# A cosine block loaded as 128 rows, half of each row product evicted by ScalarE and added on GpSimd, and the first transposes and one routing moved

## The chip, the cores and the metric

The kernel runs on one NeuronCore of one Trainium2 chip. Its engines are TensorE (PE; PEld is its weight load), VectorE (DVE), ScalarE (ACT), GpSimd (POOL) and SyncE (SP, which here only issues DMAs). Each takes its own instructions in the order in which they were written for it and waits on semaphores for the others. The metric is the device time of one execution in microseconds.

## The reference

For x of 2048 tokens and 512 features the output is a sum of three parts:

```
xn  = layernorm(x)
A   = C @ (xn @ Wre.T) - S @ (xn @ Wim.T)        # real part of a 2-D Fourier transform; C, S: 2048 x 2048 cosines, sines
q   = xn @ w_q                                   # 32 heads, two halves of 128 each
s1, s2 = q[:, :, :128] @ k1.T, q[:, :, 128:] @ k2.T        # 64 scores a half
top 2 of s1 + top 2 of s2 -> 4 candidates, best 2 -> gates g (softmax), expert indices e
B   = sum over heads and both experts of g * gelu(xn . u[e]) * v[e]   # 4096 experts
out = x + A + B
```

## The kernel before

**Layout.** Tokens are ordered so that four quarters of the sequence fold onto each other; a group g is 128 rows of each quarter, and groups are taken in the order G = (1, 0, 2, 3). Matrices named c (A in the code) are blocks of the cosine (k = 0) and sine (k = 1) matrices for one group, 128 rows of 1024 numbers, loaded by load().

**Start (to about 63 us).** For each group the layernorm is done (ln_a: statistics; ln_b: scale on ACT at L376), the quarters are folded on DVE (fold_t L412, fold_d L395 to L406, the results zq at L430 and L431), and main(k, g) multiplies the fold with the block c: eight fp32 matmuls of PE at L451 (four pairs p_00, p_10, p_01, p_11). k = 0 runs over all groups, then k = 1. Between them PE transposes the normalised rows of a group (xpose_a, L514, into banks xp; ACT copies them out at L517; xpose_b adds the low part, L525 and L527). The product of the first weights with the keys (tiles m, L145) lies in the same four PSUM banks as the first transposes until m_keep copies it out on ACT (L590). For k = 1 the block of group 0 was loaded in three pieces: 127 rows (L305), half of row 0 (L306), and the other half of row 0 from another array (row512, L296).

**Scores (63 to about 440 us).** Eight chunks j of four heads; in each, PE makes the scores of 16 token tiles i (L962, twelve matmuls into one of four banks pa), ACT copies them out (L967), DVE takes the top values (L970, L974). In between PE makes the next chunk's weights (m_mul, L141, banks of pools pc and pb, two each), from halves that ACT (L155, L160) and POOL (L163) split. The routing of a chunk (candidates, gates, indices) is done in the next chunk in three parts: part 0 (POOL L807 to L812, DVE L810, L811), part 2 (indices, POOL L829 on, DVE L826 on) and part 1, which begins with an exponential on ACT (L815). In chunk 1 the parts follow scores 9, 11 and 13 (LAG) and are held behind that score's matmuls; in the later chunks they follow scores 1, 2 and 4 and are not held.

**Row products (103 to 182 us).** Nine calls of hid put one 128-row piece each of the Fourier result in a bank (hy, pools pc and pb). Columns 0 to 256 are real parts; ACT evicts them in five pieces (L557 to L561). Columns 257 to 511 are the imaginary parts, which DVE reads from PSUM and adds to and subtracts from the real ones (L564, L565). The table HID names the score behind which each call comes: one at score 13 of chunk 0, the last at score 0 of chunk 2. y_store writes the results to DRAM ten scores later; for two of the tiles one half has rows 1 to 127 alone.

**What sets the order.** The code writes each engine's stream through a scheduler that orders instructions by its own estimate; pace, behind, hold and follow add orderings without waits between engines. The order of the queues is therefore read from the built program.

Of the kernel before, what the change touches and what calls it, by code (L numbers as in the profile page):

```python
# [16 lines left out]
ALU = mybir.AluOpType  # L17
AX = mybir.AxisListType

P = 128  # L20
# [16 lines left out]
def tile_fnet_peer(ctx, tc, x, ca, cb, c5, wt, wf, wr, wq, kt, ut, vn, uv, out):  # L37
# [257 lines left out]
    def row512(k, dst, eng=nc.sync):  # L295
        eng.dma_start(dst.rearrange("p (k c) -> p k c", k=4),  # L296
                      cb[k, 0, 4 * k:4 * k + 4, 0:1, 6:8].rearrange("k p b c -> p k (b c)"))

    def load(k, g):

        t = A[k, g] = raw_tile(f"c{k}_{g}").rearrange("p a t -> p (a t)") if k else vf[g]
        if k == 0 or g:
            nc.sync.dma_start(t, ca[k, g])
            return
        nc.sync.dma_start(t[1:P], ca[k, g, 1:P])  # L305
        nc.sync.dma_start(t[0:1, 0:512], ca[k, g, 0:1, 0:512])  # L306
        row512(k, t[0:1, 512:1024])

# [132 lines left out]

    def main(k, g, after=None):

        first, last = g == G[0], g == G[-1]
        if first:
            PP[k] = [[pa(f"p{k}_{dt}{h}") for h in range(2)] for dt in range(2)]
        for h in range(2):
            r = A[k, g][:, h * 512:(h + 1) * 512]
            l = Q[k][g][:, h ^ k]
            for dt in range(2):  # L450
                i = nc.tensor.matmul(PP[k][dt][h], l[:, dt * P:(dt + 1) * P], r, start=first, stop=last)  # L451
                if after is not None:
                    pace(i, after)

# [46 lines left out]
    XP = {}  # L501
    XL = {}

# [4 lines left out]
    def xpose_a(i, sub, after=None):  # L508

        p = XP[i] = (pb if sub and i // 4 % 2 else pc)(f"xp{i}")  # L510
        src = xn[i % 4][:, i // 4]
        for kd in range(KD):
            c = slice(kd * P, (kd + 1) * P)
            XL[0] = nc.tensor.matmul(p[:, c], src[:, c], ident, start=kd == 0, stop=kd == KD - 1 and not sub,  # L514
                                     is_transpose=True, skip_group_check=True)
        pv = p.rearrange("p (k n) -> p k n", k=KD)
        hi = nc.scalar.activation(xt[i][:, 0], pv, AF.Copy, scale=XS)  # L517
        if after is not None:
            pace(hi, after)
# [29 lines left out]

    def hid(t, n, pre, pn, pim, bank):  # L550

        nc.tensor.matmul(bank[:n, 0:129], pre[0], wfs[:, 0:129], start=True, stop=False)
        nc.tensor.matmul(bank[:n, 0:129], pn, wrs, start=False, stop=True)
        nc.tensor.matmul(bank[:n, 129:257], pre[1], wfs[:, 129:257], start=True, stop=True)
        nc.tensor.matmul(bank[:n, 257:384], pim[0], wfs[:, 257:384], start=True, stop=True)
        nc.tensor.matmul(bank[:n, 384:512], pim[1], wfs[:, 384:512], start=True, stop=True)
        nc.scalar.activation(t[:, 2:256:2], bank[:n, 0:127], AF.Copy)  # L557
        nc.scalar.activation(t[:, 1:256:2], bank[:n, 129:257], AF.Copy)
        nc.scalar.activation(t[:, 256:258], bank[:n, 127:129], AF.Copy)
        nc.scalar.activation(t[:, 513:514], bank[:n, 127:128], AF.Copy)  # L560
        nc.scalar.activation(t[:, 0:1], bank[:n, 128:129], AF.Copy)  # L561
        for a, b, im in ((2, 259, bank[:n, 257:384]), (1, 258, bank[:n, 384:512])):
            e = slice(a, 256, 2)
            nc.vector.tensor_tensor(t[:, b:513:2], t[:, e], im, op=ALU.add)  # L564
            nc.vector.tensor_tensor(t[:, e], t[:, e], im, op=ALU.subtract)  # L565

# [14 lines left out]
    for g in G:  # L581
        load(1, g)
    wfs = uf[14][:, 0:512]
# [13 lines left out]
    for n, g in enumerate(G):  # L597
# [9 lines left out]
        if n in (1, 2):  # L607
            fold_t(0, g)
            ln_a(G[n + 1], n + 1)
            if n == 1:  # L610
                OWN.append(m_keep((0, 2), ln_x(G[3], 3, SQ[2])))
            fold(0, g, AG[n + 1], lambda i: ln_b(G[n + 1], n + 1, i))
        else:
            fold(0, g)
        if n in (1, 2):
            for q in (0, 1) if n == 1 else (2, 3):
                xpose_a(4 * q + G[0], True, LN[n + 1])
        if n == 1:
            m_keep((1, 3), LN[2])
        main(0, g, XL[0] if n == 1 else None)  # L620
        if n == 0:
# [62 lines left out]
    def y_rows(n):  # L684

        if n == 8:
# [5 lines left out]
        hid(uf[n][:, 0:514], P, [PT[0][dt][h][:, c] for dt in range(2)], p256[:, h, c],  # L692
            [PT[1][dt][h][:, c] for dt in range(2)], (pb if q else pc)(f"hy{q}_{g}"))

    def y_store(n):
        if n == 8:
            t, a, b, r = uf[13][0:1, 264:778], y_d[8][0:1], y_d[12][0:1], slice(0, 1)
# [5 lines left out]
        nc.sync.dma_start(b[:, 0:256], t[r, 258:514])  # L703
        nc.sync.dma_start(b[:, 256:512], t[r, 0:256])

# [6 lines left out]
    def part_b(safe, stS, stP, stE, xt, u_sb, cmp_p):  # L712
# [316 lines left out]
        for j in range(NCH):  # L1029
# [8 lines left out]
            for i in range(NT):  # L1038
# [643 lines left out]
```

## Time and profile before

| what | us |
|---|---|
| runs of the kernel | 1081.33, 1085.77, 1083.87 (median 1083.87) |
| the profiled execution | 1083.84 |
| its span, first to last instruction | 1081.9 |
| TensorE clock granted, mean | 0.996 |
| PE busy / DVE / ACT / POOL | 1054.7 / 958.0 / 729.2 / 625.3 |

Times inside the span are counted from its start. A row of the timeline gives start, length, engine, line, operation, output and inputs, and in brackets how long the engine stood idle ahead of it and what ended that. A row of the windows gives a stretch, its length, busy time (and instructions) of PE, PEld, DVE, ACT and POOL, the granted clock of TensorE (1.00 is full), the share of the 16 DMA engines and GB/s. A row of the groups gives the count, busy time and mean length in ns, or least, median and greatest.

### The profile page before, as it was taken

The numbers are of one execution on the slowest core, as the hardware profiler recorded it, in microseconds if no ns is written. First come the engines' busy times: TensorE is split into PE (matmuls) and PEld (weight loads), VectorE is DVE, ScalarE is ACT, GpSimd is POOL, SyncE is SP. The second block draws the span as 40 slices with busy tenths as digits, with TensorE's granted clock in tenths as the row PEclk, the third lists the DMA queues.
The fourth block names the chain that finished last, engine by engine and source line by source line (L and its number), as shares of the span: only waits on it lengthen the run. The fifth ranks groups of instructions, "written<-read, shape, count | busy, mean of one in ns | idle before, by whom it ended". The sixth has DMA issues, their size and how long they took to land.

```text
span 1081.9 us, 28392 instructions
## 1 busy us (share of the span) xinstructions
PE 1054.7 (97%) x11005; PEld 688.2 (64%) x11005; DVE 958.0 (89%) x2720; ACT 729.2 (67%) x1359; POOL 625.3 (58%) x574
## 2 busy tenths in 40 slices
PE   6899998999999999999999999999999999999997
PEld 5344554454544544996785968769587685867853
DVE  7969779879999999988999998999899997999871
ACT  5787656778788757445776667666657775777641
POOL 1145646688797946225756576556566665666622
PEclk9999999999999999999999999999999999999999
DMA  8268185435445341277866767675687767666611
GB/s 334 87 152 238 64 316 174 151 136 194 156 157 184 119 137 67 86 247 223 253 192 193 214 201 231 211 233 182 189 245 210 224 209 234 213 211 212 190 31 53
DMA packets 96376, 198.87 MB, mean 184 GB/s; under 512 B 23618, under 2 KB 38999, under 8 KB 96232
## 3 DMA queue, kind: packets, MB, share of 16 engines
q1 hardware_dynamic: 75338, 125.65, 35.4%
q0 software_dynamic: 20736, 71.31, 22.5%
q8 instruction: 88, 1.44, 0.5%
q14 instruction: 56, 0.46, 0.1%
q10 hardware_dynamic: 158, 0.01, 0.0%
HBM read 176.65 MB, written 17.10 MB: 179 GB/s over the span
## 4 chain that ended last, share of the span: by engine, by line
PE 80%; DVE 8%; DMA 5%; POOL 3%; issue 2%; ACT 1%; SPq 0%; ACTq 0%; DVEq 0%; POOLq 0%
PE s L962 25%; PE z L1131 24%; PE v L1196 23%; PE g L1168 4%; DMA c<-in_ca_dram 3%; PE m L141 2%; DVE vals L970 2%; DVE idx L974 1%; PE p L451 1%; POOL ov L1256 1%; DMA wq<-in_wq_dram 1%; DVE L L1155 1%; DMA cx<-in_ca_dram 1%; DMA u<-in_c_dram 0%; POOL ga L1222 0%
## 5 line engine op out<-in xcount | busy, mean ns | idle before, releaser
L962 PE MATMUL s<-m,xq 128*128 128x512 f16 x1536 | 339.3, 380 | 0.0
L1131 PE MATMUL z<-xb,u 128*128 128x128 f16 x5376 | 306.8, 219 | 1.6 <-DVE y L1211 1.6
L1131 PEld LDWEIGHTS <-u 128*128 128x128 f16 x5376 | 301.5, 98 | 4.5 <-issue 1.6
L1196 PE MATMUL v<-v,act 128*128 128x512 f16 x1344 | 296.5, 379 | 0.0
L1256 POOL TENSOR_TENSOR ov<-ov,ga 128x512 f32<-128x512 f32 x128 | 182.5, 1426 | 184.3 <-ACT ga L1251 113.4
L962 PEld LDWEIGHTS <-xq 128*128 128x128 f16 x1536 | 148.7, 98 | 173.9 <-issue 2.6
L1196 PEld LDWEIGHTS <-act 128*128 128x128 f16 x1344 | 128.9, 98 | 149.2
L1222 POOL DMA_INDIRECT ga<-in_uv_dram,eix x128 | 160.5, 1254 | 46.2 <-POOL ov L1256 35.7
L970 DVE MAX8 vals<-ss 128x8 f32<-128x64 f32 x1024 | 152.7, 216 | 17.3 <-ACT ss L967 17.3
L1155 DVE TENSOR_TENSOR L<-io_lam,cmp 128x2048 f16<-128x2048 f16 x112 | 155.0, 1399 | 11.5 <-PE g L1168 11.4
L1134 ACT ACTIVATE act<-z,scl 128x512 f32<-128x512 f32 x112 | 75.4, 679 | 61.8 <-PE z L1131 61.3
L974 DVE FIND_INDEX8 idx<-vals,ss 128x8 uint16<-128x256 f32 x256 | 107.2, 419 | 0.0
L967 ACT ACTIVATE ss<-s,wsc 128x512 f32<-128x512 f32 x112 | 75.4, 679 | 43.4 <-PE s L962 33.9
L1251 ACT ACTIVATE ga<-ga,za 128x512 f32<-128x512 f32 x128 | 92.3, 721 | 10.1 <-ACT za L1249 0.7
L944 ACT ACTIVATE cx<-cx 128x896 f32<-128x896 f32 x64 | 60.6, 946 | 48.1 <-DVE cx L924 29.6
L1184 ACT ACTIVATE act<-g 128x1024 f16<-128x1024 f32 x56 | 73.1, 1308 | 23.5 <-DVE g L1179 23.1
L1238 DVE SCALAR_TENSOR_TENSOR ga<-ga,px 128x512 f32<-128x512 f32 x128 | 85.7, 677 | 0.1
L1187 DVE TENSOR_TENSOR act<-g,act 128x1024 f16<-128x1024 f32 x56 | 72.9, 1303 | 11.6 <-ACT act L1184 10.6
L1179 DVE SCALAR_TENSOR_TENSOR g<-act,scl,g 128x1024 f32<-128x1024 f32 x56 | 71.4, 1278 | 3.2 <-ACT act L1134 1.8
L918 POOL TENSOR_TENSOR cx<-cx 128x512 f32<-128x512 f32 (+2 forms) x48 | 53.8, 1140 | 14.0 <-DMA cx<-in_cb_dram 14.0
L918 DVE TENSOR_TENSOR cx<-cx 128x512 f32<-128x512 f32 (+2 forms) x61 | 48.5, 828 | 14.1 <-DMA cx<-in_cb_dram 14.0
L1168 PEld LDWEIGHTS <-L 128*128 128x128 f16 x1792 | 51.8, 96 | 8.5 <-DVE L L1155 1.7
(300 smaller groups left out, 1309.6 us busy)
## 6 DMA issues: line engine op xcount, KB each, us to landing
cx<-in_cb_dram SPq DMA_DIRECT2D x50, 448.0 KB
wq<-in_wq_dram SPq DMA_DIRECT2D x32, 512.0 KB
fit<-in_wq_dram SPq DMA_DIRECT2D x28, 512.0 KB
uv<-in_ut_dram SPq DMA_DIRECT2D x16, 512.0 KB
uv<-in_vn_dram SPq DMA_DIRECT2D x16, 512.0 KB
cx<-in_cb_dram SPq DMA_DIRECT2D x28, 224.0 KB
xt_d<-xq SPq DMA_DIRECT2D x16, 256.0 KB
xb<-xt_d SPq DMA_DIRECT2D x14, 256.0 KB
```

The costliest lines, as they stand in the source:

```text
L918: v_eng.tensor_tensor(v, v, tv[:, 0:1].to_broadcast([P, len(ix), 256]), op=o)
L962: mm = nc.tensor.matmul(ps, xt[i][:, l, kd, :], m[:, r, kd, :], start=(n == 0), stop=(n == 3 * KD - 1))
L970: nc.vector.max(vals[:, i, w, :, h], s[:, g, :])
L974: nc.vector.max_index(idx[:, i, w].rearrange("p k h -> p (k h)"), vals[:, i, w, 0:2].rearrange("p k h -> p (k h)"), s[:, w * HC:g + 1, :]. ...
L1131: mm = nc.tensor.matmul(p[:, cc * P:(cc + 1) * P], ug[:, l, c % 2, kd, :], xb[:, r, kd, :], start=(n == 0), stop=(n == 3 * KD - 1))
L1155: nc.vector.tensor_tensor(L.rearrange("p t (l two) -> p t l two", two=2), io_lam.rearrange("p (l two) -> p l two", two=2).unsqueeze(1).to_ ...
L1168: i = nc.tensor.matmul(p[:, hf, t * NC:(t + 1) * NC], L[:, t, :], R[:, hf * 16 + t, :], start=True, stop=True)
L1196: mm = nc.tensor.matmul(pv, w16[:, c, :, l], vg[:, r, c % 2, :], start=(c == 0 and k == 0), stop=(c == NC - 1 and k == 2))
L1222: nc.gpsimd.indirect_dma_start(out=t, out_offset=None, in_=uv, in_offset=bass.IndirectOffsetOnAxis(ap=eix[:, n].rearrange("p k h -> p (k h ...
L1238: nc.vector.scalar_tensor_tensor(t, t, 1.0, T["x"], op0=ALU.mult, op1=ALU.mult, accum_out=T["z", n][:, s:s + 1])
L1251: nc.scalar.activation(t, t, AF.Copy, scale=z)
L1256: T["a"] = nc.gpsimd.tensor_tensor(o, o, t, op=ALU.add)
```

## The change

Four things. The 127-row load becomes one of 128 rows, like the other blocks; row512 then overwrites half of row 0, placed behind the load of the last group. In hid, for the eight full tiles, ACT copies columns 257 to 511 of the bank into the free part of the same tile (s), and the four additions run on POOL from there. The transposes of the first group come after the third group's statistics instead of beside the second's, and all four copies of m_keep go with them. The routing that runs in chunk 2 follows scores 9, 11 and 13 and is held, as in chunk 1. Stores of rows 1 to 127 are split at row 64.

```diff
     def load(k, g):
         t = A[k, g] = raw_tile(f"c{k}_{g}").rearrange("p a t -> p (a t)") if k else vf[g]
-        if k == 0 or g:
-            nc.sync.dma_start(t, ca[k, g])
-            return
-        nc.sync.dma_start(t[1:P], ca[k, g, 1:P])
-        nc.sync.dma_start(t[0:1, 0:512], ca[k, g, 0:1, 0:512])
-        row512(k, t[0:1, 512:1024])
+        return nc.sync.dma_start(t, ca[k, g])
...
     for g in G:
-        load(1, g)
+        last = load(1, g)
+    pace(row512(1, A[1, 0][0:1, 512:1024]), last)
...
-    def hid(t, n, pre, pn, pim, bank):
+    def hid(t, n, pre, pn, pim, bank, s=None):
...
-        for a, b, im in ((2, 259, bank[:n, 257:384]), (1, 258, bank[:n, 384:512])):
+        im, eng = bank[:n, 257:512], nc.vector
+        if s is not None:
+            nc.scalar.activation(s, im, AF.Copy)
+            im, eng = s, nc.gpsimd
+        for a, b, v in ((2, 259, im[:, 0:127]), (1, 258, im[:, 127:255])):
             e = slice(a, 256, 2)
-            nc.vector.tensor_tensor(t[:, b:513:2], t[:, e], im, op=ALU.add)
-            nc.vector.tensor_tensor(t[:, e], t[:, e], im, op=ALU.subtract)
+            eng.tensor_tensor(t[:, b:513:2], t[:, e], v, op=ALU.add)
+            eng.tensor_tensor(t[:, e], t[:, e], v, op=ALU.subtract)
...
             if n == 1:
-                OWN.append(m_keep((0, 2), ln_x(G[3], 3, SQ[2])))
+                OWN.append(ln_x(G[3], 3, SQ[2]))
+            else:
+                m_keep(range(KD), SQ[3])
+                for q in (0, 1):
+                    xpose_a(4 * q + G[0], True, LN[2])
             fold(0, g, AG[n + 1], lambda i: ln_b(G[n + 1], n + 1, i))
...
-        if n in (1, 2):
-            for q in (0, 1) if n == 1 else (2, 3):
-                xpose_a(4 * q + G[0], True, LN[n + 1])
-        if n == 1:
-            m_keep((1, 3), LN[2])
-        main(0, g, XL[0] if n == 1 else None)
+        if n == 2:
+            for q in (2, 3):
+                xpose_a(4 * q + G[0], True, LN[3])
+        main(0, g)
...
-            r = slice(0 if g else 1, P)
-            t, a, b = uf[n][:, 0:514], y_d[4 * q + g], y_d[4 * q + 8 + g][r]
+            rows = [slice(0, P)] if g else [slice(1, 64), slice(64, P)]
+            t, a, b = uf[n][:, 0:514], y_d[4 * q + g], y_d[4 * q + 8 + g]
...
-                if j == 1 and not safe:
+                if j in (1, 2) and not safe:
                     if i in LAG:
```

What this makes of the queues, at three places. SP's loads of the sine blocks (c_1, c_0, c_2, c_3 are those of groups 1, 0, 2, 3), before:

```order
L303 DMA c_1_184<-in_ca_dram 128x1024
L305 DMA c_0_186<-in_ca_dram 127x1024
L306 DMA c_0_186<-in_ca_dram 1x512
L296 DMA c_0_186<-in_cb_dram 1x4x128
L303 DMA c_2_190<-in_ca_dram 128x1024
L303 DMA c_3_192<-in_ca_dram 128x1024
L584 DMA u_127<-in_wf_dram 128x512
```

and now:

```order
L302 DMA c_1_184<-in_ca_dram 128x1024
L302 DMA c_0_186<-in_ca_dram 128x1024
L302 DMA c_2_188<-in_ca_dram 128x1024
L302 DMA c_3_190<-in_ca_dram 128x1024
L296 DMA c_0_186<-in_cb_dram 1x4x128
L581 DMA u_127<-in_wf_dram 128x512
```

One load of 128 rows takes the place of two, and the half row from the other array (L296) goes behind the load of group 3.

ACT in the start, from the last step of the statistics of group 3 (mvs) on; m are the products that m_keep copies, xq_102 and xq_103 the rows of groups 2 and 3 that are normalised, xp the transposes of the first group. Before:

```order
L339 ACTIVATE mvs<-sx_317 128x1
L590 ACTIVATE u_115<-m_0_196 128x512
L338 ACTIVATE mvs<-sx_317 128x1
L590 ACTIVATE u_116<-m_2_252 128x512
L376 ACTIVATE xq_102<-xq_102,negm,rstd 128x512 x4
L517 ACTIVATE xq_101<-xp_343 128x512
L517 ACTIVATE xq_101<-xp_349 128x512
L590 ACTIVATE u_115<-m_1_199 128x512
L590 ACTIVATE u_116<-m_3_255 128x512
L353 ACTIVATE sm_369<-mvs,eps 128x4
L376 ACTIVATE xq_103<-xq_103,negm,rstd 128x512 x4
```

and now:

```order
L371 ACTIVATE xq_102<-xq_102,negm,rstd 128x512
L333 ACTIVATE mvs<-sx_316 128x1
L371 ACTIVATE xq_102<-xq_102,negm,rstd 128x512 x3
L348 ACTIVATE sm_352<-mvs,eps 128x4
L587 ACTIVATE u_115<-m_0_195 128x512
L587 ACTIVATE u_115<-m_1_198 128x512
L587 ACTIVATE u_116<-m_2_251 128x512
L587 ACTIVATE u_116<-m_3_254 128x512
L509 ACTIVATE xq_101<-xp_358 128x512
L509 ACTIVATE xq_101<-xp_364 128x512
L371 ACTIVATE xq_103<-xq_103,negm,rstd 128x512 x4
```

The normalisation of group 2 and the square root of group 3 (sm) move ahead of all four copies of m. On PE, nine transposes of group 0 (before, six) now stand between the two halves of main(1, 0).

ACT at the start of chunk 2, from the eviction of score 0 (ss_0) and the last row product (hy_3) on. Before:

```order
L967 ACTIVATE ss_0_2013<-s_0_2000,wsc 128x512
L557 ACTIVATE u_120<-hy_3_2025 128x127
L558 ACTIVATE u_120<-hy_3_2025 128x128
L559 ACTIVATE u_120<-hy_3_2025 128x2
L560 ACTIVATE u_120<-hy_3_2025 128x1
L561 ACTIVATE u_120<-hy_3_2025 128x1
L815 ACTIVATE c_0_2070<-c_0_2068 128x64
L182 ACTIVATE m_2419,sums<-m_1665 128x2048
L967 ACTIVATE ss_1_2053<-s_1_2040,wsc 128x512
```

and now:

```order
L967 ACTIVATE ss_0_2023<-s_0_2010,wsc 128x512
L549 ACTIVATE u_120<-hy_3_2035 128x127
L550 ACTIVATE u_120<-hy_3_2035 128x128
L551 ACTIVATE u_120<-hy_3_2035 128x2
L552 ACTIVATE u_120<-hy_3_2035 128x1
L553 ACTIVATE u_120<-hy_3_2035 128x1
L556 ACTIVATE u_120<-hy_3_2035 128x255
L182 ACTIVATE m_2390,sums<-m_1669 128x2048
L967 ACTIVATE ss_1_2064<-s_1_2051,wsc 128x512
```

The exponential of the routing (L815) is gone from here; it now stands ahead of the eviction of score 13. The copy of the bank's second half (L556) is new, and the four DVE additions for this tile are gone from DVE's queue and stand on POOL's.

More of the change, by code (lines that the diff above doesn't have):

```diff
@@ L440, in tile_fnet_peer, with main @@
     PP = {}
-    def main(k, g, after=None):
+    def main(k, g):
         first, last = g == G[0], g == G[-1]
@@ L450, in main @@
             for dt in range(2):
-                i = nc.tensor.matmul(PP[k][dt][h], l[:, dt * P:(dt + 1) * P], r, start=first, stop=last)
-                if after is not None:
-                    pace(i, after)
+                nc.tensor.matmul(PP[k][dt][h], l[:, dt * P:(dt + 1) * P], r, start=first, stop=last)
     def main_row():
@@ L513, in xpose_a @@
             c = slice(kd * P, (kd + 1) * P)
-            XL[0] = nc.tensor.matmul(p[:, c], src[:, c], ident, start=kd == 0, stop=kd == KD - 1 and not sub,
-                                     is_transpose=True, skip_group_check=True)
+            nc.tensor.matmul(p[:, c], src[:, c], ident, start=kd == 0, stop=kd == KD - 1 and not sub,
+                             is_transpose=True, skip_group_check=True)
         pv = p.rearrange("p (k n) -> p k n", k=KD)
```

12 lines of the change are left out of this document (6 added, 6 removed).

## The prediction

> **What bounds the kernel now.** I read the page first for the engine that is full, then windows by stage for where it is not, then the waits and the timeline around each hole.
>
> ```profile
> span 1081.9 us, 28392 instructions
> ...
> PE 1054.7 (97%) x11005; PEld 688.2 (64%) x11005; DVE 958.0 (89%) x2720; ACT 729.2 (67%) x1359; POOL 625.3 (58%) x574
> ...
> PE 80%; DVE 8%; DMA 5%; POOL 3%; issue 2%; ACT 1%; SPq 0%; ACTq 0%; DVEq 0%; POOLq 0%
> ```
>
> PE is busy 97% and makes up 80% of the chain that ended last. DVE's 89% matters only where it leaves PE without work. The windows say where that is (length, then busy time of PE, PEld, DVE, ACT, POOL, then the granted clock):
>
> ```profile
> 107.55:151.80 44.25, 44.25 (x302) 24.23 (x301) 33.13 (x187) 25.28 (x58) 22.08 (x20) 1.00 0.44 144
> 151.80:196.05 44.25, 41.22 (x269) 22.32 (x268) 40.84 (x200) 28.28 (x53) 32.22 (x43) 0.96 0.61 221
> 196.05:240.30 44.25, 44.25 (x295) 21.61 (x291) 34.12 (x182) 34.41 (x45) 29.43 (x32) 1.00 0.37 125
> ...
> 284.55:328.80 44.25, 44.25 (x295) 21.60 (x292) 41.50 (x211) 36.26 (x50) 36.36 (x41) 1.00 0.49 167
> ...
> 600.00:700.00 100.00, 100.00 (x1404) 77.34 (x1402) 92.41 (x132) 70.72 (x150) 60.29 (x47) 1.00 0.73 219
> ```
>
> From 63.3 us, where the scores begin, PE has no hole except one between 151.8 and 196 (3.03 us idle, and a low clock), and it is full through the routing and the expert part. So whatever makes PE reach the scores earlier, and whatever closes that hole, passes to the end in full; DVE, ACT or POOL time saved elsewhere is worth nothing. Two places count.
>
> **The hole at 179 to 186 us.**
>
> ```profile
> 182.35 0.26 PE L141 MATMUL m<-sums,wh 128*128 128x64 f16 x2 [3.03 <-DVE u L565]
> 186.57 0.22 PE L141 MATMUL m<-sums,wh 128*128 128x64 f16 x2
> 189.86 0.22 PE L141 MATMUL m<-sums,wh 128*128 128x64 f16 x2
> ...
> 178.15 0.26 ACT L815 ACTIVATE c<-c 128x64 f32<-128x64 f32 x1 [5.26 <-POOL c L812]
> ...
> 175.11 2.13 POOL L163 TENSOR_TENSOR wq<-wq,wh 128x1024 f16<-128x1024 f32 x1
> 175.19 2.13 DVE L810 TENSOR_TENSOR pm<-c,c 128x64 f32<-128x64 f32 x1 [0.45 <-POOL c L809]
> 177.45 0.21 DVE L811 TENSOR_TENSOR c<-c,c 128x64 f32<-128x64 f32 x1
> 177.80 0.32 POOL L812 TENSOR_TENSOR c<-c,c 128x64 f32<-128x64 f32 x1 [0.56 <-DVE c L811]
> 181.92 0.28 DVE L565 TENSOR_TENSOR u<-u,hy 128x128 f32<-128x128 f32 x1
> ```
>
> PE waits 3.03 us for the PSUM bank of the last row product, which DVE's L565 empties at 182.20. DVE is that late because the routing of chunk 1's scores stands in front of it: L810, which is 0.21 long when it runs alone like L811, ran 2.13 beside POOL's 2.13 L163; that delayed POOL's L812, for which the exponential L815 held ACT's queue 5.26 us, and with it the score evictions that DVE works on. After the hole the same block (16 short matmul groups and 12 long ones) took 182.35 to 186.57 = 4.22, against 186.57 to 189.86 = 3.29 for the next one: 0.93 more is the clock. The hole costs 3.03 + 0.93 = 3.96.
>
> The change attacks it twice. ACT now copies columns 257 to 511 of each bank, directly behind the five evictions, which ended at 178.15 - 5.26 = 172.9, so that the bank is free near 173.3, 6 us before PE asks; and the routing, with its L815, moves to scores 9, 11 and 13 of that chunk, so that nothing holds ACT there. Either would nearly do. I take the whole 3.96; bounds 0 (a new wait in the same place) and 3.96.
>
> What this adds lies beside PE:
>
> ```profile
> L490 ACT ACTIVATE u<-p x6: 569/578/597, 61.5 to 101.8; 128x512 f32<-128x512 f32 x4, 1x512 f32<-1x512 f32 x2
> L558 ACT ACTIVATE u<-hy x9: 257/283/382, 107.4 to 172.4; 128x128 f32<-128x128 f32 x8, 1x128 f32<-1x128 f32 x1
> ...
> L924 POOL TENSOR_TENSOR cx<-cx 128x128 f32<-128x128 f32 x7 | 3.2, 454 | 7.3 <-issue 6.9
> L564 DVE TENSOR_TENSOR u<-u,hy 128x128 f32<-128x128 f32 x8 | 2.3, 283 | 0.0
> L822 DVE TENSOR_TENSOR zq<-g,zq 128x128 f16<-128x128 f32 x2 | 2.5, 1228 | 0.0
> ...
> L811 DVE TENSOR_TENSOR c<-c,c 128x64 f32<-128x64 f32 x2 | 0.4, 218 | 0.0
> ```
>
> - ACT: 8 copies of 128x255, between 0.283 (128 columns) and 0.578 (512); at 0.38 it is 3 us, in windows with 16 to 19 us free. Zero. Behind each copy the next score eviction waits 0.38; four score banks cover 10 us.
> - POOL: 32 adds at 0.454 = 14.5 us, 5.4 of them in the window with 22.08 busy, 9.1 in the one with 32.22, which loses one routing's POOL work. Zero. The weight splits (L163) queue behind each block of four adds, 1.8 us; they feed matmuls several scores later.
> - DVE loses 32 adds at about 0.28 = 9 us; no gain by itself, since PE is full.
> - The routing's DVE part enters 196 to 240. Its fourteen groups, from L822 (2.5 us for two routings) down to L811 (0.4), sum to 7.5 us for one: 34.12 + 7.5 = 41.6 of 44.25, what 284 to 329 carries (41.50) with PE full. Zero, with 2.6 us of cover left.
> - Rows 1 to 63 and 64 to 127 stored apart: four more stores on SP, which PE doesn't wait for. Zero.
>
> [...] The rows give 454 against 283, 1.6x. [...]
>
> **The start, 17 to 63 us.**
>
> ```profile
> 33.00 3.70 PE L451 MATMUL p<-v,zq 128*128 128x512 f32 x8 [1.51 <-DVE zq L430]
> 30.00:40.00 10.00, 8.32 (x27) 3.78 (x27) 9.05 (x25) 8.48 (x17) 1.71 (x3) 1.00 0.41 147
> ...
> 17.27 0.30 SPq L305 DMA_DIRECT2D c<-in_ca_dram  x1
> 18.55 29.69 DMA c<-in_ca_dram
> 42.84 3.60 PE L451 MATMUL p<-c,zq 128*128 128x512 f32 x8
> 45.49 0.42 DVE L431 TENSOR_TENSOR zq<-fo 128x255 f32<-128x255 f32 x1
> 47.00:48.00 1.00, 0.00 (x0) 0.00 (x0) 1.00 (x4) 1.00 (x4) 0.00 (x0) 1.00 0.07 27
> 48.38 3.30 PE L451 MATMUL p<-c,zq 128*128 128x512 f32 x4 [1.93 <-DMA c<-in_ca_dram]
> 48.76 0.27 DVE L406 TENSOR_TENSOR zq<-r 1x127 f32<-1x127 f32 x1
> 49.00:50.00 1.00, 1.00 (x3) 0.48 (x2) 0.96 (x5) 0.06 (x1) 0.00 (x0) 0.50 0.06 25
> 52.49 0.60 ACT L517 ACTIVATE xq<-xp 128x512 f16<-128x512 f32 x1 [3.43 <-PE xp L514]
> 52.51 1.88 PE L451 MATMUL p<-c,zq 128*128 128x512 f32 x4
> 54.45 1.25 PE L514 MATMUL xp<-ident,xq 128*128 128x128 f32 x10
> 63.29 13.11 PE L962 MATMUL s<-m,xq 128*128 128x512 f16 x60
> ```
>
> The 127-row load is issued at 17.27 and lands at 18.55 + 29.69 = 48.24; around it the DMA share is 0.06 to 0.07, one engine of 16, at 25 to 27 GB/s. PE is done with the block before at 46.44, its DVE operand is there at 45.91, so only the load holds it, 1.93 us, and then PE runs at clock 0.50.
>
> Loaded as 128 rows, the block comes with its neighbours, far ahead of 46. Then the first four matmuls run from 46.44 for 1.80 (half of the eight's 3.60) to 48.24; nine transposes stand next on PE at 0.125 each (1.25 / 10), 1.13, to 49.37; DVE's first-row fix is ready at 49.03. The second four start at 49.37 instead of 52.51: 3.14 earlier. What is late next is ACT: its idle 3.43 goes, but in the new order two more copies stand ahead of transposes that PE waits for; I take 0.4 off: 2.7. The row's own DMA now waits on SP for the block and for the slot behind group 3's load; the weights of the row products queue behind it, first read behind chunk 0's thirteenth score, so that costs nothing.
>
> ```profile
> 25.92 2.92 ACT L376 ACTIVATE xq<-xq,negm,rstd 128x512 f32<-128x512 f32 x4
> 28.87 1.23 DVE L412 TENSOR_TENSOR ft<-xq 128x1024 f32<-128x1024 f32 x1 [0.47 <-ACT xq L376]
> 35.40 1.23 DVE L412 TENSOR_TENSOR ft<-xq 128x1024 f32<-128x1024 f32 x1 [0.51 <-ACT xq L376]
> ```
>
> The first group turned later: two copies leave the front of the normalisation at 25.92, so DVE's 0.47 goes; the four copies and two evictions then stand before the next normalisation, so of its 0.51 about 0.3 goes. DVE is otherwise packed from 28 to 56 us, so this term is 0.3, between 0 and 0.98. Start: 2.7 + 0.3 = 3.0, bounds 1.2 (below) and 4.0.
>
> **Sum.** The profiled execution took 1083.84 (span 1081.9 and 1.9 around it), the median of the runs is 1083.87, so it stands for them. 1083.84 - 3.96 - 3.0 = 1076.9.
>
> **Rivals.**
> - *The low clock stays.* If the slow stretch after 48.4 has another cause than the idle, its (3.30 - 1.80) + 0.3 = 1.8 us stay and the start gives 1.2: 1078.7. For it: the idle of 1.51 us ahead of 33.00 left the clock at 1.00. Against: it fell to 0.50 right behind the idles of 1.93 and 3.03, and nowhere else after 10 us. Chance 0.13. [...]
> - *A new wait takes the hole's place.* POOL, with 14.5 us more, becomes the one that ACT or a bank waits for, near 150 to 215 us; only the start gains: 1080.8. Against: the free POOL and DVE time above. Chance 0.10.
> - *It does not do what it says:* DVE's packed fold binds the start and the hole returns with the routing around 205 us: 1083 to 1084. Chance 0.04.
> - *Slower.* The adds and L163 hold DVE instructions as L163 held L810 (2.13 for 0.21) in eight blocks of 1.8 us. Once that and the routing put DVE more than the four score banks (4 x 13.11 / 5 = 10 us) behind, PE stops as at 182, 4 us each time; two stops and no gain there give 1083.84 - 3.0 + 8 = 1088.8. Against: DVE had 11 us free in 107 to 152 and gets 9 more. Chance 0.04.
>
> **How the numbers follow.** The forecast, both gains, has 0.69, its own span 1075 to 1079. The range of 8 in 10 reaches from 1074.8 (start at its upper bound, 4.0, and 1 us from small holes that PE has behind DVE after 500 us) to 1081.0, which takes in the first two rivals. A measurement tells 0.5% from no change, which is 1078.4. Below it lies most of the forecast and some of the first rival: faster 0.67; same 0.29; slower 0.04.
>
> **What would show it.** PE: no idle above 0.5 us between 42 and 60 us, clock 1.00 there, first scores near 60.3 instead of 63.29; the load landed before 35 us. At chunk 2's third score no wait on a row product's bank, clock 1.00; POOL adds near 0.45. ACT's wait at L815 is short and stands near score 13. Wrong would be: a PE wait on ACT's transposed evictions near 52 us, a PE hole between 150 and 215 us, or PE no longer full after 450 us.

## The result, and the profile after

| | before | after |
|---|---|---|
| median of 8 runs, us | 1085.30 | 1079.36 |
| lowest and highest | 1081.33, 1090.98 | 1077.06, 1082.57 |
| ratio, with its 95% interval | | 0.9944 (0.9916 to 0.9971) |
| the profiled execution, and its span | 1083.84, 1081.9 | 1081.48, 1079.4 |
| first matmul to first score ("start") | 53.98 | 49.92 |
| first score to first expert matmul ("stretch") | 372.61 | 369.93 |
| first expert matmul to the end ("experts") | 646.00 | 650.39 |

The changed kernel is faster by 0.56%, 5.9 us between medians. The three parts in the lower rows are read from the starts of three instructions on PE (before 9.31, 63.29, 435.90; after 9.16, 59.08, 429.01), and they are what the experiments are compared by. The part from the first score on that the change touches repeats to about 0.1 us; the last part does not, as will be seen. One timed run each of two later experiments (e1 and e8) took 1367 and 1819 us at a low granted clock (0.753 and 0.56 in the mean), and is left out.

The head of the page, as it was shown of before:

```profile
span 1079.4 us, 28396 instructions
PE 1055.1 (98%) x11005; PEld 689.3 (64%) x11005; DVE 943.0 (87%) x2688; ACT 732.0 (68%) x1367; POOL 637.3 (59%) x606
PE 78%; DVE 10%; POOL 4%; DMA 2%; issue 2%; ACT 2%; SPq 0%; DVEq 0%; POOLq 0%; ACTq 0%
```

DVE lost 15 us of work and POOL gained 12; PE is as busy as before, in a shorter span. The windows over the middle of the scores (same columns as before):

```profile
107.55:151.80 44.25, 44.25 (x302) 24.22 (x301) 30.18 (x168) 27.04 (x64) 32.37 (x46) 1.00 0.63 218
151.80:196.05 44.25, 44.25 (x299) 23.59 (x298) 32.26 (x186) 32.27 (x57) 32.89 (x41) 1.00 0.51 176
196.05:240.30 44.25, 43.84 (x287) 21.32 (x286) 36.85 (x188) 33.20 (x46) 37.08 (x45) 1.00 0.40 135
```

The hole of 3.03 us is gone, and the clock is 1.00 throughout. A smaller hole, 44.25 - 43.84 = 0.41, stands in the next window. One number there matters later: the DMA share between 107 and 152 us was 0.44 and is 0.63.

PE's waits, in order of time, from the timeline of PE:

```profile
25.34 5.18 PE L446 MATMUL p<-v,zq 128*128 128x512 f32 x8 [1.10 <-DVE zq L425]
42.46 5.39 PE L446 MATMUL p<-c,zq 128*128 128x512 f32 x12
59.08 5.13 PE L962 MATMUL s<-m,xq 128*128 128x512 f16 x23
237.57 2.75 PE L962 MATMUL s<-m,xq 128*128 128x512 f16 x12 [0.41 <-ACT ss L967]
410.27 5.97 PE L962 MATMUL s<-m,xq 128*128 128x512 f16 x26 [0.96 <-ACT ss L967]
444.02 0.56 PE L1168 MATMUL g<-R,L 128*128 128x32 f16 x16 [1.05 <-DVE L L1155]
782.07 2.18 PE L1131 MATMUL z<-xb,u 128*128 128x128 f16 x24 [2.58 <-DVE y L1211]
```

And ACT's waits at the routing's exponential, from the timeline of ACT:

```profile
220.50 0.26 ACT L815 ACTIVATE c<-c 128x64 f32<-128x64 f32 x1 [6.23 <-POOL c L812]
396.42 0.26 ACT L815 ACTIVATE c<-c 128x64 f32<-128x64 f32 x1 [7.11 <-POOL c L812]
409.43 0.21 ACT L815 ACTIVATE c<-c 128x16 f32<-128x16 f32 x1 [5.08 <-DVE c L812]
```

PE runs through the sine blocks without a stop (twelve matmuls in one row at 42.46), and it has two new waits on score evictions, 0.41 and 0.96. In front of each stands ACT, held in its own queue: before 237.57 by POOL's check of a cosine block (the kernel tests the symmetry of these blocks, tiles cx; L944, 4.69 at 235.91), before 410.27 by the exponential at 409.43. ACT's wait at the moved exponential is gone, as forecast (it runs at 203.60 with no wait); but the next routing's, at 220.50, has grown from 2.97 in before to 6.23. The clock of the start did not stay full; it fell elsewhere (windows of 2 us):

```profile
24.00:26.00 2.00, 0.90 (x4) 0.60 (x3) 1.90 (x8) 1.96 (x6) 0.00 (x0) 0.73 1.01 404
26.00:28.00 2.00, 2.00 (x3) 0.66 (x2) 1.86 (x6) 1.80 (x3) 0.00 (x0) 0.50 1.05 416
```

What was added, as groups:

```profile
L556 ACT ACTIVATE u<-hy 128x255 f32<-128x255 f32 x8 | 3.6, 453 | 0.0
L560 POOL TENSOR_TENSOR u<-u 128x127 f32<-128x127 f32 (+1 forms) x16 | 7.2, 471 | 3.0 <-ACT u L556 3.0
```

The copies take 3.6 us and the additions 2 x 7.2, about as estimated.

The section on the change counts four things; the split stores, its last sentence, are a fifth, and they turn out to matter most.

By the first expert matmul the change had gained 6.89 us (435.90 - 429.01), of which the profiled execution showed only 2.5 at its end: its last part, the same code, took 4.39 us longer. So two questions stand: is that loss the change's, and which of its parts made the gain?

### The profile page after: what moved, and what is told of

It is laid out like the page before. It is cut to its first block, busy times and chain, and to the rows that moved or that the text cites. A ratio compares the mean times of both kernels' runs of the same rounds, so it can differ in the third digit from the quotient of the medians.

```text
span 1079.4 us, 28396 instructions
## 1 busy us (share of the span) xinstructions
PE 1055.1 (98%) x11005; PEld 689.3 (64%) x11005; DVE 943.0 (87%) x2688; ACT 732.0 (68%) x1367; POOL 637.3 (59%) x606
## 4 chain that ended last, share of the span: by engine, by line
PE 78%; DVE 10%; POOL 4%; DMA 2%; issue 2%; ACT 2%; SPq 0%; DVEq 0%; POOLq 0%; ACTq 0%
PE z L1131 23%; PE v L1196 23%; PE s L962 22%; PE g L1168 3%; PE p L446 2%; DVE vals L970 2%; DVE idx L974 2%; PE m L141 1%; DVE L L1155 1%; POOL ov L1256 1%; DMA fit<-in_wq_dram 1%; DVE cx L918 1%; DMA cx<-in_cb_dram 1%; POOL u L764 1%; DMA cx<-in_ca_dram 0%
## 5 line engine op out<-in xcount | busy, mean ns | idle before, releaser
L1256 POOL TENSOR_TENSOR ov<-ov,ga 128x512 f32<-128x512 f32 x128 | 185.9, 1453 | 189.7 <-ACT ga L1251 118.7
L1222 POOL DMA_INDIRECT ga<-in_uv_dram,eix x128 | 156.3, 1221 | 46.3 <-POOL ov L1256 34.5
L1155 DVE TENSOR_TENSOR L<-io_lam,cmp 128x2048 f16<-128x2048 f16 x112 | 149.7, 1352 | 16.6 <-PE g L1168 16.4
L944 ACT ACTIVATE cx<-cx 128x896 f32<-128x896 f32 x64 | 60.7, 948 | 62.3 <-DVE cx L924 36.7
L918 DVE TENSOR_TENSOR cx<-cx 128x512 f32<-128x512 f32 (+2 forms) x61 | 48.1, 821 | 13.2 <-DMA cx<-in_cb_dram 12.4
L1168 PE MATMUL g<-R,L 128*128 128x32 f16 x1792 | 53.8, 176 | 2.8 <-DVE L L1155 2.3
```

What stands on the lines that cost most here:

```text
L1155: nc.vector.tensor_tensor(L.rearrange("p t (l two) -> p t l two", two=2), io_lam.rearrange("p (l two) -> p l two", two=2).unsqueeze(1).to_ ...
L1168: i = nc.tensor.matmul(p[:, hf, t * NC:(t + 1) * NC], L[:, t, :], R[:, hf * 16 + t, :], start=True, stop=True)
L1222: nc.gpsimd.indirect_dma_start(out=t, out_offset=None, in_=uv, in_offset=bass.IndirectOffsetOnAxis(ap=eix[:, n].rearrange("p k h -> p (k h ...
L1256: T["a"] = nc.gpsimd.tensor_tensor(o, o, t, op=ALU.add)
```

## The experiments

All times in us; n is the number of timed runs, and the ratio is to the kernel before on the same chip.

| run | start | stretch | experts | median (n) | ratio (95%) |
|---|---|---|---|---|---|
| before | 53.98 | 372.61 | 646.00 | | |
| after | 49.92 | 369.93 | 650.39 | 1079.36 (8) | 0.9944 (0.9916 to 0.9971) |
| e1_load | 50.48 | 374.42 | 651.54 | 1084.68 (9) | 0.9992 (0.9976 to 1.0009) |
| e2_pool | 52.06 | 369.69 | 649.17 | 1083.95 (10) | 0.9987 (0.9968 to 1.0006) |
| e3_lag | 52.50 | 369.84 | 650.62 | 1083.34 (10) | 0.9980 (0.9961 to 0.9999) |
| e4_after | 49.32 | 369.93 | 648.78 | 1077.83 (4) | 0.9929 (0.9905 to 0.9952) |
| e5_earlier | 50.65 | 370.02 | 648.81 | 1080.54 (3) | 0.9944 (0.9917 to 0.9970) |
| e6_dveadd | 49.26 | 370.06 | 648.82 | 1078.69 (2) | 0.9922 (0.9892 to 0.9952) |
| e7_nolag | 50.34 | 367.96 | 648.51 | 1078.76 (2) | 0.9922 (0.9893 to 0.9952) |
| e8_exp | 51.54 | 368.53 | 658.49 | 1089.12 (9) | 1.0026 (1.0008 to 1.0044) |
| e9_split | 54.58 | 367.95 | 647.29 | 1080.80 (10) | 0.9957 (0.9940 to 0.9974) |
| e10_nopool | 50.33 | 367.95 | 646.22 | 1075.28 (4) | 0.9903 (0.9877 to 0.9929) |
| e11_nolag | 49.44 | 367.95 | 650.44 | 1075.17 (6) | 0.9908 (0.9885 to 0.9930) |
| e12_whole | 49.11 | 370.30 | 655.41 | 1080.71 (8) | 0.9949 (0.9931 to 0.9967) |

### Each part alone: e1_load, e2_pool, e3_lag

e1 has the load alone:

```diff
-        nc.sync.dma_start(t[1:P], ca[k, g, 1:P])
-        nc.sync.dma_start(t[0:1, 0:512], ca[k, g, 0:1, 0:512])
-        row512(k, t[0:1, 512:1024])
+        return nc.sync.dma_start(t, ca[k, g])
...
+    pace(row512(1, A[1, 0][0:1, 512:1024]), last)
```

> The kernel before with the 128-row load alone (and the half row behind group 3's load); hid, the first group's transposes and the routing stay. Measured by the start of the first score matmul (63.29 us before, 59.08 after) and, behind it, by the stretch from there to the first expert matmul (372.6 before, 369.9 after). Theory: the load is nearly all of the start's gain, by the wait of 1.93 us and the low clock behind it; no PE wait near 48 us, first score at 59.2 to 60.0, the stretch stays at 372.6 with the hole of about 3 us near 178. Rival 1: the low clock has another cause than the idle and stays: first score near 62.1. Rival 2: the first group turned later made half of the gain: first score near 61.3.

First score at 60.04, no wait near 48: the theory for the start holds. The stretch did not stay. PE, 3 us earlier, met a larger hole at the same bank:

```profile
179.60 0.27 PE L141 MATMUL m<-sums,wh 128*128 128x64 f16 x2 [3.53 <-DVE u L560]
```

(L560 is the L565 of before.) The low clock there lasted twice as long, 6.83 us instead of 3.41, so that only 1.4 us were left at the first expert matmul (434.46 against 435.90).

e2 has the copy and the additions on GpSimd alone, e3 the moved routing alone:

```diff
+        if s is not None:
+            nc.scalar.activation(s, im, AF.Copy)
+            im, eng = s, nc.gpsimd
```

> The kernel before with the ScalarE copy of the banks' second halves and the additions on GpSimd alone. Theory: the bank of the last row product is then free before PE asks, although the routing still stands at scores 1, 2 and 4 and ACT is still held at the exponential: no PE wait on a row product's bank near 182 us, the stretch from first score to first expert matmul falls from 372.6 by 3 to 4 us to about 369; the first score stays at 63.3. Rival: what holds PE is DVE and ACT behind the routing, not the bank: the hole moves to a wait on score evictions and the stretch stays within 1 us of 372.6.

```diff
-                if j == 1 and not safe:
+                if j in (1, 2) and not safe:
                     if i in LAG:
```

> The kernel before with the routing in chunk 2 at scores 9, 11 and 13 alone; the additions stay on DVE and read PSUM. Theory: with no routing in front of L565 the bank is free in time and the hole closes as well: the stretch from first score to first expert matmul falls from 372.6 by 3 to 4 us; PE has a new wait of at most 0.5 us near 237, as the changed kernel has (0.41). Rival: DVE, which still carries the 32 additions, is late anyway, and PE keeps a wait of 1 us or more on L565.

Either closes the hole: 369.69 and 369.84, against 372.61. Both have the small waits, 0.19 and 0.36 near 240, 0.95 and 0.94 near 412, so these do not come from the moved routing alone. The start of e3 held a surprise. Its code there is that of before. The timeline of PE:

```profile
48.51 1.96 PE L451 MATMUL p<-c,zq 128*128 128x512 f32 x4 [1.91 <-DMA c<-in_ca_dram]
```

The windows there:

```profile
48.00:50.00 2.00, 1.49 (x4) 0.81 (x5) 1.97 (x9) 1.23 (x4) 0.00 (x0) 1.00 0.06 25
50.00:52.00 2.00, 2.00 (x11) 1.23 (x10) 1.92 (x4) 1.06 (x2) 0.98 (x1) 1.00 0.07 25
```

PE waits 1.91 for the load (1.93 before), and the clock stays at 1.00: the four matmuls take 1.96 instead of 3.30. So the low clock behind the load is not a fixed part of this program. It made 53.98 of a start that is 52.50 without it. (e2, with the same load, has 52.06: its clock fell at 25.8 instead, PE's later waits took that up, and at 48.41 it waited 1.57.)

### What repeats: e4_after

No edit.

> The changed kernel once more, nothing edited, for what repeats from one execution to the next. Theory: the start and the scores repeat (first score 59.1, first expert matmul 429.0, both within 0.3 us), and the expert part, which took 650.4 us in the changed kernel's profile and 646.0 in the one before, differs by executions: it comes out somewhere between 644 and 652 and its waits near 782 and 801 us have other lengths. Rival: the change slows the expert part (by what it leaves late on POOL or DVE): again 650 or more, with the same waits at the same places.

The stretch repeats to 0.01 us. The start is 49.32, as PE's first wait was 0.72 and the clock stayed at 1.00. The experts took 648.78; over all runs but e8 they took 646.0 to 655.4, also where only the start was edited (e1: 651.54). So most of the 4.39 us lost behind the scores is the difference of two executions: the wait of 2.58 at 782.07 is 1.87 in e4 and 1.55 in before, and the clock fell behind it in nine of the fourteen profiles, in that of after (to 0.50 at 782.69) but not in that of before. But the rival is right in part. PE's wait at 444.02 was shorter in before:

```profile
450.06 0.56 PE L1168 MATMUL g<-R,L 128*128 128x32 f16 x16 [0.20 <-DVE L L1155]
```

It is 1.03 to 1.05 in after, e2 to e6 and e12, and 0.20 to 0.33 in before, e1, e7 and e9 to e11. That difference, about 0.85, repeats, and it comes with the small waits near 237 and 410.

### The parts inside the changed kernel: e5_earlier to e8_exp

e5 has the first group as early as before, and whole stores:

```diff
-                m_keep(range(KD), SQ[3])
-                for q in (0, 1):
-                    xpose_a(4 * q + G[0], True, LN[2])
...
+        main(0, g, XL[0] if n == 1 else None)
```

> The changed kernel with the first group turned as early as before and the stores whole: the load, the additions on GpSimd and the moved routing stay. Starts are counted from the first matmul (9.31 us in the kernel before), since that one waits for the first load alone. Theory: behind an undisturbed clock the first score comes 52.5 us after it in the kernel before (the run with the routing alone), 50.4 with the load alone and 49.3 in the changed kernel (its second profile); so turning the first group later is worth about 1.1 us and this kernel has 50.4, as with the load alone. Rival: it is worth the 0.3 us of the prediction, and this kernel has 49.6. A low clock in the start adds up to 1.8 us to either and shows in the clock. The stretch from first score to first expert matmul is that of the changed kernel by both, 369.9.

The start is 50.65 at full clock, by the theory: turning the first group later is worth 1.3 us (50.48 and 50.65, against 49.32, 49.26 and 49.44).

e6 has the additions on DVE, from the copy:

```diff
-            im, eng = s, nc.gpsimd
+            im, eng = s, nc.vector
```

> The changed kernel with the 32 additions back on DVE, now from the copy in SBUF; ScalarE still empties the banks. Theory: the bank decides, not the engine that adds; with the additions on either engine PE has no wait on a row product, and the 9 us more on DVE lie in windows where it has room: the stretch from first score to first expert matmul is 369.9 within 0.4, with the same small waits near 237 and 410. Rival: DVE's room is what the change bought, and the stretch grows by 1 us or more by waits on score evictions between 110 and 240 us or by longer ones at 237 and 410.

370.06 (369.93 with them on GpSimd): the engine that adds made no difference. The additions take 19.0 us on DVE here (9.0 in before, from PSUM), and the 14.8 us on POOL are gone; neither counts.

e7 has the routing of chunk 2 back at scores 1, 2 and 4:

```diff
-                if j in (1, 2) and not safe:
+                if j == 1 and not safe:
                     if i in LAG:
```

> The changed kernel with the routing in chunk 2 at scores 1, 2 and 4 as before. Theory: with the banks emptied by ScalarE the move of the routing is worth nothing: stretch 369.7 as in the run with the additions alone, wait near 237 at 0.2 instead of 0.4. Rival: the move protects PE once it runs ahead of DVE by the start's gain: PE waits 1 us or more between 170 and 190.

Both were wrong: PE had no wait at all in the scores, and the stretch was 367.96, so the move of the routing cost 2 us. But e2, with the routing in its old place too, had the waits. What e7 has and e2 lacks is the start and the split stores.

e8 has the small routing's exponential two scores later:

```diff
-                    for part in range(3):
+                    for part in (0, 2):
                         routing(part, j, vals, idx, 0, 4, nc.vector)
+                if j + 1 == NCH and i == 6:
+                    hold(lambda: routing(1, j, vals, idx, 0, 4, nc.vector), mm)
```

> The changed kernel with one more move: in the last chunk the exponential of the small routing of its first four tiles stands two scores later, behind score 6 instead of score 4, held there. ScalarE waited 5.1 us at it with the score evictions behind it, and PE then waited 0.96 to 1.01 us near 410 (it did not in the kernel before, where PE came 6 us later in time). Theory: ScalarE's wait at that exponential makes PE's wait: it goes, the stretch falls from 369.9 to about 369.0, and the time by 1 us at most. Rival: DVE, with 64 of 67 us busy there, is the bound once PE runs ahead, and PE waits as long for an eviction in the same chunk, whatever the exponential does.

The wait near 410 is gone (stretch 368.53): ACT's wait at that exponential made it. The time is 0.26% above before all the same, by the experts' 658.49. Three of PE's holes there, from its timeline:

```profile
445.73 0.58 PE L1170 MATMUL g<-R,L 128*128 128x32 f16 x16 [2.23 <-DVE R L1168]
448.53 0.61 PE L1170 MATMUL g<-R,L 128*128 128x32 f16 x16 [2.23 <-DVE L L1157]
459.95 0.59 PE L1133 MATMUL z<-xb,u 128*128 128x128 f16 x4 [1.03 <-issue]
```

PE has seven holes between 435 and 462: two behind DVE, one behind ACT, and four for which the profile names nothing ("issue"). The clock was at 0.50 for 6.83 us twice there, from 445.8 and from 459.5. Which move in the queues made the holes was not traced.

### The stores: e9_split to e12_whole

Between e2 and e7 the difference starts on SP, not on a compute engine: e2's stores held SP for 5 to 7 us each. The same stands in the profile of before, in SP's timeline, and the prediction passed over it:

```profile
118.36 6.13 SPq L703 DMA_DIRECT2D y_d<-u  x1
124.55 5.29 SPq L1048 DMA_DIRECT2D xt_d<-xq  x1
130.71 5.71 SPq L1048 DMA_DIRECT2D xt_d<-xq  x1
142.43 0.72 SPq L131 DMA_DIRECT2D wq<-in_wq_dram  x1
```

POOL's timeline at that time:

```profile
145.77 1.95 POOL L918 TENSOR_TENSOR cx<-cx 128x512 f32<-128x512 f32 x2 [14.00 <-DMA cx<-in_cb_dram]
```

And the window in which SP stands:

```profile
120.00:130.00 10.00, 10.00 (x69) 4.92 (x68) 8.67 (x52) 5.36 (x11) 8.99 (x7) 1.00 0.07 25
```

While the stores of 127 rows are under way the share is 0.07 (one engine of sixteen is 0.0625), at 25 GB/s, and three issues of SP between 118 and 137 us take 5.29 to 6.13 us instead of 0.3 to 0.5. The weights behind (L131) leave at 142.43. POOL's check of a cosine block (L918) waits 14 us for its load, and the routing stands behind that check in POOL's queue.

e9 splits the stores of the kernel before, and nothing else:

```diff
-        nc.sync.dma_start(b[:, 0:256], t[r, 258:514])
-        nc.sync.dma_start(b[:, 256:512], t[r, 0:256])
+        for r in rows:
+            nc.sync.dma_start(b[r, 0:256], t[r, 258:514])
+            nc.sync.dma_start(b[r, 256:512], t[r, 0:256])
```

> The kernel before with the stores of rows 1 to 127 split at row 64 alone. In the kernels with whole stores SP stands for 5 to 7 us at each of two to three of them between 115 and 140 us, and the loads of the next weights, queued behind, start 15 us later than with split stores; GpSimd and DVE then work off chunk 0's routing and the weight splits late. Theory: these stores are the root of the wait at 182: without them no SP issue above 2 us, DMA share between 120 and 130 us near 0.7 instead of 0.07, and PE's wait on the bank is gone or under 1 us; stretch from first score to first expert matmul 368 to 369.5 instead of 372.6. Rival: the routing in front of DVE's additions is the cause by itself, and the wait near 182 stays at 2 us or more.

The four lines of before to look at, from the timelines of DVE and POOL (L810 at 148.99 and L845 and L822 belong to the routing of chunk 0, L807 begins that of chunk 1):

```profile
148.99 0.23 DVE L810 TENSOR_TENSOR pm<-c,c 128x64 f32<-128x64 f32 x1 [2.31 <-POOL c L809]
160.32 1.58 DVE L845 TENSOR_SCALAR eix<-di 128x16 int32<-128x16 int32 x1
168.14 2.03 DVE L822 TENSOR_TENSOR zq<-g,zq 128x128 f16<-128x128 f32 x1
174.28 0.32 POOL L807 TENSOR_TENSOR c<-vals 128x64 f32<-128x64 f32 x1 [4.27 <-DVE vals L970]
```

And e9, from the timelines of SP, DVE, POOL and ACT (lines from L703 on stand one higher in this kernel):

```profile
128.15 0.33 SPq L131 DMA_DIRECT2D wq<-in_wq_dram  x1
146.97 0.21 DVE L811 TENSOR_TENSOR pm<-c,c 128x64 f32<-128x64 f32 x1
170.26 0.32 POOL L808 TENSOR_TENSOR c<-vals 128x64 f32<-128x64 f32 x1 [1.55 <-DVE vals L971]
171.22 2.17 POOL L163 TENSOR_TENSOR wq<-wq,wh 128x1024 f16<-128x1024 f32 x1
171.18 0.23 DVE L811 TENSOR_TENSOR pm<-c,c 128x64 f32<-128x64 f32 x1 [0.46 <-POOL c L810]
171.32 2.22 DVE L827 CAST if<-idx 128x256 f32<-128x256 uint16 x1
173.82 0.32 POOL L813 TENSOR_TENSOR c<-c,c 128x64 f32<-128x64 f32 x1 [0.43 <-DVE c L812]
174.17 0.26 ACT L816 ACTIVATE c<-c 128x64 f32<-128x64 f32 x1 [0.91 <-POOL c L813]
```

The same window as above:

```profile
120.00:130.00 10.00, 10.00 (x69) 4.93 (x68) 8.53 (x52) 6.32 (x15) 9.55 (x8) 1.00 0.70 221
```

The loads leave 12 to 14 us earlier and the DMA share is 0.70. POOL does not wait for its check any more, so the routing of chunk 0 reaches DVE 2.0 us earlier (146.97 for 148.99), and two later steps of it that lay beside POOL's long steps in before (L845 and L822, 1.58 and 2.03) take 0.17 and 0.29. So the routing of chunk 1 begins 4.0 us earlier (170.26 for 174.28), and ACT's hold of 5.26 is 0.91.

What did not go is the stretched step that the prediction named. Here it is the next instruction of DVE, L827, that takes 2.22 beside POOL's L163, and from the routing's first POOL step to POOL's L813 it is 3.56 us, as it was in before (174.28 to 177.80, 3.52). The routing is as slow as before; it only comes in time.

PE has no wait from the first score to the first expert matmul. The stretch is 367.95, and the time 0.43% below before, with a start (54.58) that is no better. Up to there DVE, ACT and POOL work off the same instructions in the same order as in before; only SP's queue differs. The theory holds and the rival falls.

e10 leaves the changed kernel its load, its first group and its split stores, and takes the copy, the GpSimd additions and the moved routing back:

```diff
-        if s is not None:
-            nc.scalar.activation(s, im, AF.Copy)
-            im, eng = s, nc.gpsimd
...
-                if j in (1, 2) and not safe:
+                if j == 1 and not safe:
```

> The changed kernel without the copy and the additions on GpSimd (they are on DVE from PSUM as before) and without the moved routing: what is left is the load, the first group turned later and the split stores. Theory: split stores alone close the hole, so the stretch is 368 to 369.5 here too, and the whole gain comes from three changes of DMAs and order; first score 49.3 us after the first matmul at full clock. Rival: without the copy the bank is late once PE comes 4 us earlier, and PE waits 2 us or more on L565's bank near 178.

e11 keeps the copy and the additions and takes only the moved routing back (the kernel of e7):

> The changed kernel with the routing of chunk 2 back at scores 1, 2 and 4, a second time and over more rounds. Its first run had no PE wait at all between the first score and the first expert matmul (stretch 368.0; the changed kernel 369.9). Theory: that repeats, and the move of the routing costs the changed kernel 1.9 us: this one is 1 to 2 us faster, ratio to the kernel before 0.991 to 0.994. Rival: the first run's start was late by a low clock and PE so came later to its small waits: with an undisturbed start they are back, and the stretch is 369.5 or more.

Both have 367.95 and no wait on PE there. The start of e11 is at full clock; that of e10 is 50.33, not 49.3, with the clock at 0.50 behind a wait of 1.43. So the copy and the additions on GpSimd add nothing once the stores are split, and the moved routing costs 369.93 - 367.95 = 1.98, and the 0.85 at 444 besides. e10 and e11 have the lowest medians, 1075.28 and 1075.17. Against before both are clearly faster; against the changed kernel their intervals overlap with its, so that only the stretch and that wait tell the cost.

e12 is e11 with the stores whole:

```diff
-            rows = [slice(0, P)] if g else [slice(1, 64), slice(64, P)]
+            r = slice(0 if g else 1, P)
```

> The kernel of the run before this one, with the stores of rows 1 to 127 whole again. Theory: SP stands at them for 5 to 7 us each, weights come 15 us later, and PE's small waits near 238 and 410 are back, as in the run with the additions alone: stretch 369.7. Rival: those waits there had to do with the start, not with the stores; stretch 368.0.

SP's timeline (lines stand one lower in this kernel):

```profile
117.78 6.20 SPq L702 DMA_DIRECT2D y_d<-u  x1
124.09 5.98 SPq L701 DMA_DIRECT2D y_d<-u  x1
142.77 0.38 SPq L131 DMA_DIRECT2D wq<-in_wq_dram  x1
```

PE's timeline:

```profile
237.25 2.96 PE L961 MATMUL s<-m,xq 128*128 128x512 f16 x13 [0.35 <-ACT ss L966]
409.95 6.41 PE L961 MATMUL s<-m,xq 128*128 128x512 f16 x28 [0.97 <-ACT ss L966]
```

SP stands again, and PE's waits are back (a third, of 0.27, near 178), with 370.30. The stores, not the start, told e2 and e7 apart.

## Why the prediction was right, and where its steps were not

The forecast was 1076.9, the range 1074.8 to 1081.0; 1079.36 was measured, and a gain of 5.9 us for 7.0. (Of the 2.5 us between them, 1.4 lie in the base: 1083.87 by three runs, 1085.30 by eight.) By the first expert matmul the profiles have 6.89. The sum came out near because errors of its steps cancel, and that was luck: the load gave 0.7 less than forecast, the first group 1.0 more, the hole 0.7 more, and the moved routing took 2.0.

**What bounds the kernel** was right: what PE gained at the start and at the hole reached the first expert matmul, and DVE's and POOL's time alone was worth nothing (e6). With the hole open a gain at the start does not pass in full: of e1's 3.5, 1.4 were left.

**The start, 3.0.** Full clock against full clock it is 52.50 to 49.3, 3.2, but not in the forecast's parts. The load is worth 2.0 (52.50 to about 50.5; 1.6 by e2's 52.06), not 2.7; the first group 1.3, not 0.3. The 2.7 counted the slow matmuls after 48.4 as the load's own; e3 has the load's wait without them. The 0.3 was taken from DVE's waits alone. PE's own had stood in the same rows: between 20 and 36 us it waits 1.68 with the first group early (e5: 0.17 and 1.51) and 0.72 with it late (e4). That is 0.96 of the 1.3; the rest was not traced. In the profiled pair the start gave 4.06, as the low clock of before cost 1.5 and that of after 0.6.

**The hole, 3.96.** It closed, and "either would nearly do" was right (e2, e3). Without any hole the stretch is 367.95, so it had cost 4.66. Most of the 0.7 between them is the low clock, 0.93 in the sum: the prediction compared two blocks as the same that are not. The wait stood behind 12 of the 16 groups of short matmuls of its block. The 12 long ones alone tell it, in before:

```profile
182.64 4.10 PE L962 MATMUL s<-m,xq 128*128 128x512 f16 x12
187.27 2.75 PE L962 MATMUL s<-m,xq 128*128 128x512 f16 x12
```

That is 1.35; set side by side with e9, where the same matmuls run at full clock, it is 1.46 with the short ones.

Of the cause named, ACT's hold at L815 is a link (5.26, and 0.91 in e9), but L810 stretched beside L163 did not decide: a step is stretched there in e9 too (L827, 2.22) and in e10 (2.22 at 167.07), and PE has no wait. What decided is that the routing came 4 us late, and the first link of that is the whole stores. So the step that failed is the last bullet of that part: "four more stores on SP, which PE doesn't wait for. Zero." Alone the split stores are worth all 4.66 (e9). Beside the moved routing they are worth nothing (e5: 370.02), and without it 2.35 (e12 to e11). The prediction had the twin of it in its hands: it read in the start that 127 rows came in at a share of 0.06 to 0.07, one engine of 16, and 25 to 27 GB/s, and did not look for other transfers of 127 rows. Nor did it look at what SP did behind that load: its next issue stood 14.19 us (at 18.55).

**The moved routing at zero, "with 2.6 us of cover left".** It costs 1.98 in the stretch: the window was asked for its busy time and not for its order. DVE's index step of the next routing, from DVE's timeline, in the changed kernel:

```profile
220.22 0.42 DVE L831 TENSOR_REDUCE bnd<-if 128x1 f32<-128x256 f32 x1 [0.59 <-POOL if L829]
```

and in e11:

```profile
216.72 0.42 DVE L831 TENSOR_REDUCE bnd<-if 128x1 f32<-128x256 f32 x1 [0.59 <-POOL if L829]
```

From the first score it is 161.1 us away in one and 157.7 in the other: DVE comes 3.4 us later out of that window. From there on it is nearly full and does not catch up: at the end of the scores it is still 2.8 us later. So POOL's check that holds ACT ahead of 237.57 ends 3.5 us later from the first score than in e11 (235.91 and 232.38), the exponential ahead of 410.27 stands 2.8 us later (409.43 and 406.56), and PE, which is not later, meets both. Set side by side with e11, matmul by matmul, the 1.98 opens at these two scores, 0.58 and 1.12, and in two steps of 0.2 and 0.1 within 10 us behind the second.

**The additions** on GpSimd and the copies at zero were right, at 0.47 an addition: the stretch was the same on either engine (369.93 on GpSimd, 370.06 on DVE in e6).

**The rivals.** "The low clock stays" was right in part: the same wait came with it (1.93 in before) and without it (1.91 in e3), so the idle alone did not decide it. "A new wait takes the hole's place" came in part, 1.4 us of waits, later than it was looked for. The third and the fourth did not occur.

## What to carry to other kernels

Look at the queue that issues the DMAs as you look at an engine: an issue that lasted 6 us instead of 0.4 was a wait here, and what it delayed showed 50 us later, on engines that seemed to be in each other's way. When the transfer of one shape turns out slow (here 127 rows), look for all others of that shape. Where several edits each close the same hole, test each alone and then take each away: here one of them did all of it, and of the two others, once it was in, one was worth nothing and one cost 2 to 3 us. And when a hole closes, check that the step blamed for it has changed: here it had not.

## What the runs showed of the hardware

**One DMA engine for 127 rows.** Load and store alike: a share of 0.06 to 0.07 of the sixteen engines (one is 0.0625), 25 to 27 GB/s, and the queue behind stood 5.29 to 6.20 us a store (before, e12) and 14.19 us at the load (before). Split into 63 and 64 rows (e9), no issue of these stores took over 0.71 us, and the share between 120 and 130 us was 0.70.

**The clock fell at short idles, and not each time.** It went to 0.50 at idles of PE of 0.79 (e8), 1.10 (after), 1.43 (e10), 1.93 (before) and 2.40 us (e9), and stayed at 1.00 at 1.51 (before, e1, e3, e5), 1.57 (e2) and 1.91 (e3).

The low stretches themselves have a pattern. In before and after, up to the last microseconds of the kernel, each lasts 3.41 us, and the two in one execution begin a whole multiple of 3.413 us apart: in before at 48.84 and 181.96 (39 times), in after at 24.93 and 782.69 (222 times). The two of 6.83 us in e8 begin 4 times that apart (445.8 and 459.5). Where an idle lay on such a grid did not decide alone: the 1.93 of before lay within one step (45.43 to 48.84), the 1.51 of before and the 1.10 of after each across a border (31.77 and 24.93), and the clock fell with the first and the third, not with the second.

**DVE additions beside GpSimd.** In e6, with both inputs in SBUF, the sixteen additions of L560 took 272 to 2218 ns, 288 in the median, the long ones beside POOL instructions of about 2 us. With one input in PSUM the 36 additions took 256 to 291 ns in before and 256 to 307 ns in e10, also beside such POOL instructions (in before those from 117.20 to 118.03 beside L163, 2.1 each): none took longer.
